# Attention plus mixer on one core: head by feature halves, feature-permuted u, keys and values of batches 4 to 7 summed over two DMAs, 8 KB rows of w_ch2, and a new order of all steps

## The chip, the core and the metric

The kernel runs on one core of a Trainium2 chip. A core has engines with a queue of their own each: TensorE (PE in the profile, its weight loads PEld), VectorE (DVE), ScalarE (ACT), GpSimd (POOL) and SyncE (SP). Matrix products land in PSUM, from where DVE or ACT move them on; DMAs move data between HBM and SBUF and are issued here from SP, ACT and POOL. Within an engine instructions run in program order; between engines they wait on semaphores. The metric is the device time of one execution in microseconds (us), lower is better.

## What is computed

```
k_p, v_p = k, v averaged over groups of 8 rows           # 576 -> 72 rows, per head
x   = softmax(q k_p^T / 8) v_p, heads side by side       # [8 batches, 576, 512]
h   = relu(x^T w_tok1) w_tok2                            # token mixing, 256 hidden
u   = x + h^T
out = u + relu(u w_ch1) w_ch2                            # channel mixing, 1536 hidden
```

q, k and v are [8, 8, 576, 64], w_tok1 [576, 256], w_tok2 [256, 576], w_ch1 [512, 1536], w_ch2 [1536, 512]; all are fp32 in HBM and bf16 in SBUF.

## The kernel before

**Units.** The program has a head and nine units. The head brings in the first data and takes batch 0 through attention and token mixing. Unit n (0 to 7) does the channel mixing of rows 0 to 511 of batch n, and unit 8 that of the last 64 rows of all batches together (`u_tails`). Each unit is a Python generator that yields after every few matmuls: a first stage of 12 tiles (`l1_tile`, L515: four matmuls 128x512 each, then a ReLU on ACT into `GT`, L519), two yields a tile, slots 0 to 23; then a second stage. In units 0 to 2 (`unit_plain`) that is 48 matmuls 128x512 (L538), with the residual added on DVE (L544). From unit 3 on (`unit_fast`) it is a product of seven block products with 84 matmuls 128x256 (L587), which needs sums of weight blocks (`weight_sum`, steps W, L558/L565) and of blocks of `GT` (`g_sums`, steps =), made on DVE, and adds with `plus` (L608).

**Order by hand.** At each yield, `unit` looks into `PLANS[n]` and issues the steps listed for that slot: steps of batch n+1 without a mark, of batch n with `<`, of batch n+2 with `>`. The text of the plan therefore is the order on all engines; the queue of each engine is in that order. `HEAD` is the same for batch 0. The steps:

- `lk lv lq` load keys, values, queries on the queue of POOL; `+k +v` issue one more accumulating DMA (`add_rows`, L140).
- `K0 K1 V0 V1` pool keys and values on POOL, `k1`, `v0`, `v1` on DVE. Batches 1 to 3 add eight rows in three operations (`pool8`, L203, L204, L207/L209). For batches 4 to 7 (`SUMMED = 4`) the rows are added by the DMAs: four DMAs a tensor, each of which brings a pair of the eight rows to fp32 sums in SBUF, and one DVE/POOL addition is left (L255). A DMA adds to what the one before it wrote, so POOL waits for each before it issues the next.
- `kpT` transposes the pooled keys on PE (L261), `Q0 Q1` transpose queries on DVE (L310), `s0` to `s3` are scores and exponentials (L321, L327), `av0` to `av4` attention times values and the division (L359, L371, L377), `at0 at1` the first token product and its ReLU (L405, L396), `u0` to `u4` the second and the sum u (L420, L421).
- u must be turned before the first stage: on PE for early batches (`t0` to `t4`, L430, L431); later through HBM: `M0 M2 M4` spill u and `M` reads it back in another order (both on SP's queue), `T0` to `T4` finish with block transposes on DVE (L453).

Batch 0 is different: keys and values are pooled on PE with the identity as weights (L270, L292), the head waits for nothing but its loads, u is turned by accumulating x and the token product transposed (`X0..3`, `A0..3`, L469, L477), and `d` steps are matmuls on a zero tile that keep PE busy (L662).

**Buffers.** PSUM pools: `ps_one` four one-bank tiles, `ps_two` two two-bank tiles. Raw keys, values, queries: two buffers each.

**u's layout.** Feature 4m+k of u stands at column 4m+k. `w_ch1` is loaded with four neighbouring rows on one partition, so the k-th quarter of the contraction is every fourth column of u.

Of the kernel before, what the change touches and what calls it, by code (L numbers as in the profile page):

```python
# [8 lines left out]
FP32 = mybir.dt.float32  # L9
# [6 lines left out]
FAST = 3  # L16
POOLE = mybir.EngineType.Pool
# [5 lines left out]
HEAD = """c0 c1 d8 q0 d1 q1 d5 kp0 kp1 kt0 d2 o0 e0 kt1 kp2 kp3 o1 e1 kt2 kt3 q2 q3 d2 o2 e2 vpool0 o3 d1 vpool1 e3 d2  # L23
          aw1 av0 av2 d2 av3 at_0 at_2 av4 at_1 at_3 d2 at_4 X0 X1 X2 A0 A1 A2 X3 A3 d3"""
PLANS = {
    0: {0: "K0", 1: "<u0", 4: "<u3", 5: "k1 Q1", 12: "V0", 15: "<u1 lv2", 18: "kpT", 19: "Q0 s2 v1",
        20: "<u2 lq3 s0", 22: "s3", 24: "s1", 25: "lv3", 26: "av1", 27: "av3 av2", 29: "lk3 av0", 30: ">K1",
        33: "av4", 34: "at1", 35: "at0", 36: "u4", 37: "u3 u2", 38: "u1", 39: ">K0 t4", 42: "t1", 43: "u0",
        44: "t2 t3", 45: "t0 >V1 >V0"},
    1: {0: "kpT", 1: "lk3", 2: "Q1", 4: "Q0", 8: "s0", 9: "lv3", 11: "s1", 14: "s2", 18: "s3", 19: ">K0", 20: "av1",  # L30
        21: "av3 >Q1", 23: "+k3a +v3a", 24: "av2", 26: "av0", 28: "av4", 29: ">K1", 30: "at1 +k3b at0",
        31: ">kpT >v0", 33: ">s2", 34: ">Q0 u0", 35: "u1", 37: "+v3b", 38: ">s3 u3", 40: "lq3 t1 t3", 41: "+k3c",
        42: ">V1 u2", 43: "lk4 +v3c", 44: ">s0 t2", 46: "t0", 47: ">s1"},
    2: {2: "av4 >K1", 3: "av3 >K0", 6: "av2 lv3", 8: "+k3a lq3", 10: "av0", 12: "av1", 13: ">Q0 >kpT", 14: "at1",
        16: "at0 >Q1", 18: "+v3a >s0", 19: "u3", 20: ">s2", 25: "u1 >V0", 26: "W00", 27: "t3 t1 >s1", 28: "W01 u0",
        29: "W02 +k3b u4", 30: "W10 u2", 32: "W03 >s3", 33: ">V1", 37: "+v3b >av0 >av2", 38: "t0", 39: "t2 >av4 W11",
        41: "W13", 43: "+k3c", 45: ">av1", 46: ">av3 t4", 47: "+v3c lv4"},
    3: {0: "lk3 >Q1", 1: ">K1 W12", 3: "at1", 5: ">K0", 9: "at0", 10: ">kpT", 11: "u3", 12: "u1 >s2", 13: "u0",
        14: "M0 >Q0", 15: "u2 M2", 16: "M +v3a lq3", 17: ">V0", 18: ">s1 =1a =2a", 22: "=3b", 23: "=1b =2b",
        25: ">s3 =4a", 27: ">V1 +v3b", 28: ">s0", 29: "+k3a", 31: "=4b", 32: "=3a >av2", 36: ">av1", 37: "+k3b",  # L40
        39: ">av0 T2", 40: "T1 T0 T3", 43: ">av4 >av3"},
    4: {1: ">Q1", 4: "+v2c at0", 5: "+k2c at1", 6: "lv3", 7: ">K0 u4 M4 >K1 lk3", 8: "u2 u3 M2 u0", 10: ">Q0",
        11: "u1", 12: ">kpT +v3a", 14: ">s2", 17: ">s1", 19: "+k3a M0", 20: "=1a =2a", 21: ">s3", 22: "=4a =3a",
        25: "=1b", 26: ">V0 M", 27: "=2b >s0", 29: "+v3b", 30: "=4b =3b", 31: ">V1", 33: ">av0", 35: "T1 lq3 >av1",
        36: ">av2 T0 T2", 37: "+k3b", 39: "T3", 43: "+k3c", 44: ">av3"},
    5: {2: "<T4 av4", 5: ">Q1 >K1", 6: "at0 at1", 8: ">K0 +v2c", 10: "u0 u1", 11: "u3", 12: ">kpT >Q0", 14: "M0",
        15: ">s2", 16: "u2 M2", 17: "=3a >s1", 18: "=1a", 19: "M =2a", 21: ">V1", 25: "=3b >s3 =1b =2b", 28: "=4a",
        29: "=4b", 31: ">s0", 33: "T2", 34: ">V0 >av0", 35: ">av1", 38: "T1", 39: ">av2 T0", 40: "T3", 41: ">av3",
        43: ">av4"},
    6: {4: "at0", 5: "at1", 6: "u4", 7: "u0 u2 u1", 8: "u3", 9: "M4", 10: "M2", 12: "M0", 14: "=3a", 16: "=3b",  # L50
        17: "M", 18: "=1a", 19: "=2a", 21: "=4a", 25: "=1b", 31: "=2b", 32: "T2 =4b", 34: "T1", 37: "T3", 39: "T0",
        44: "T4"},
    7: {7: "=3a", 16: "=3b", 19: "=1a =2a", 21: "=4a", 27: "=1b =2b", 36: "=4b"},
    8: {7: "=3a", 17: "=1a", 18: "=2a", 19: "=4a", 22: "=3b", 24: "=1b", 26: "=2b", 30: "=4b"},
# [4 lines left out]
def kernel(  # L59
# [45 lines left out]
    w_ch1 = singles.tile([P, 4, DC], BF16)  # L105
# [26 lines left out]
    def pair_sums(b, key):  # L132
        return loaded[b, key].rearrange("j h i d -> j (h i d)").bitcast(FP32)[:, 0:H * 2 * D].rearrange(
            "j (h n) -> j h n", h=H)

    def add_rows(b, key):
        i = parts_of[b, key]
        parts_of[b, key] = i + 1
        src = (k if key == "k" else v)[b].rearrange("h (j i) d -> j h (i d)", i=POOL)
        nc.gpsimd.dma_start(out=pair_sums(b, key), in_=src[:, :, 2 * i * D:2 * (i + 1) * D],  # L140
                            accum_op=ALU.add if i else ALU.bypass)
# [12 lines left out]

    def load_q(b):
        qb = loaded[b, "q"] = raw.tile([P, HP, BR * D + D], BF16, name="qb")
        if b == 0:
            nc.vector.memset(qb[:, :, BR * D:], 0.0)
            nc.gpsimd.dma_start(out=qb[:, 2:HP, 0:BR * D], in_=q_pairs(2, HP))
        else:  # L160
            nc.gpsimd.dma_start(out=quarters(qb), in_=q[b].rearrange("(g l) (j n) d -> (l j) g (n d)", l=4, n=2 * BR))
# [8 lines left out]
    def load_tok():  # L170
        nc.gpsimd.dma_start(out=f2, in_=moe_w_tok2.rearrange("(c p) n -> p c n", p=P))
        w = moe_w_tok1.rearrange("(p r) n -> p r n", r=BR)
        for half in range(2):
            rows = slice(half * BP, (half + 1) * BP)
            nc.gpsimd.dma_start(out=w_tok1[rows, 0:4, :],
                                in_=w[:, 0:8, :].rearrange("p (c u) n -> p c u n", u=2)[:, :, half])
        for half in range(2):
            rows = slice(half * BP, (half + 1) * BP)
            nc.gpsimd.dma_start(out=w_tok1[rows, 4 + half, :], in_=w[:, 8, :])

    def permute_tok2():
        src = f2.rearrange("t m (p r) -> t m r p", r=BR)
        dst = w_tok2.rearrange("t m (r p) -> t m r p", p=BP)
        for m in range(2):
            nc.gpsimd.tensor_copy(out=dst[:, m], in_=src[:, m])
# [3 lines left out]
    def load_ch1():  # L189
        for g in range(3):  # L190
            cols = slice(g * 512, (g + 1) * 512)
            nc.gpsimd.dma_start(out=w_ch1[:, :, cols], in_=moe_w_ch1[:, cols].rearrange("(p c) n -> p c n", c=4))

    def load_ch2(gs):
        for g in gs:
            nc.gpsimd.dma_start(out=w_ch2[:, 4 * g:4 * g + 4, :],
                                in_=moe_w_ch2[g * 512:(g + 1) * 512, :].rearrange("(c p) n -> p c n", p=P))
# [13 lines left out]
    tails = {}  # L211

    def batch_steps(b):
# [26 lines left out]
        def parts(src):  # L240
            return src.rearrange("p (m k) -> p k m", k=4)

        def pool(eng, t, g):
            def go():
# [5 lines left out]
                pair = pair_sums(b, t)[:, hs].rearrange("j l (i n) -> i j l n", i=2)  # L250
# [14 lines left out]
        def kp2(a):  # L265
            def go():
# [6 lines left out]
                (nc.scalar.copy if a == 1 else nc.vector.tensor_copy)(out=kpz[:, hs, 0:4:3, :], in_=view)  # L273
            return go

        def kt2(a):
            def go():
# [6 lines left out]
                nc.vector.tensor_copy(out=kT[:, :, 2 * a * SP:(2 * a + 2) * SP], in_=ps.rearrange("m o h j -> m o (h j)"))  # L284
            return go

        def ppool(g):
            def go():
                ps = ps_one.tile([P, 512], FP32, name="p1")
                hs = slice(g * HP, (g + 1) * HP)  # L290
                for i in range(POOL):
                    nc.tensor.matmul(out=ps[0:SP, 0:HP * D], lhsT=ident[0:SP, 0:SP], rhs=loaded[b, "v"][:, hs, i, :],  # L292
                                     start=(i == 0), stop=(i == POOL - 1))
                view = ps[0:SP, 0:HP * D].rearrange("j (h d) -> j h d", d=D)
                nc.vector.tensor_copy(out=st["vp"][:, hs, 0:D], in_=view)
# [50 lines left out]
        def av(c, act=False):  # L346
            def go():
# [5 lines left out]
                if first and c == 2:  # L353
                    halves = [ps_one.tile([P, 512], FP32, name="p1") for _ in range(2)]
                else:
                    ps = ps_two.tile([P, 2, 512], FP32, name="p2")
                    halves = [ps[:, 0], ps[:, 1]]
                for h in range(H):
                    nc.tensor.matmul(out=halves[h // 4][:, (h % 4) * (D + 1):(h % 4 + 1) * (D + 1)],  # L359
                                     lhsT=st["ex"][:, h * S + n0:h * S + n0 + P], rhs=st["vp"][:, h, :],  # L360
                                     start=True, stop=True)
                if first and c == 2:
                    for a in range(2):
                        view = halves[a][:, 0:4 * (D + 1)].rearrange("p (h e) -> p h e", e=D + 1)
# [388 lines left out]
```

## Time and profile before

| | before |
|---|---|
| median of 3 runs | 280.47 us (278.95 to 281.81) |
| the profiled execution | 280.81 us, of which the span in the profile is 279.0 us |
| PE, DVE, ACT, POOL busy | 264.5, 172.6, 113.4, 119.5 us |
| DMA | 37.47 MB landed, HBM read 38.21 MB |
| q0 (DMAs issued by POOL) | 32112 packets, 55.4% of 16 engines |

The span is what the profile covers; 1.8 us of the execution lie outside it. "Busy" of PE includes the latency of each matmul, so that short gaps between matmuls do not show in it. The first weight load of the first stage stands in the timeline at 24.81 us, and those of units 1 to 8 at 58.90, 90.28, 121.35, 148.26, 177.59, 208.72, 233.50 and 253.55 us; they cut the span into head and units. A line of a timeline is: start, length, engine, line and operation, out<-in, shape, count, and in brackets the idle time before it and what ended it. A line of the waits is: who waited, for whom, us in total, times, longest.

### The profile page before, as it was taken

The numbers are of one execution on the slowest core, as the hardware profiler recorded it, in microseconds if no ns is written. First come the engines' busy times: TensorE is split into PE (matmuls) and PEld (weight loads), VectorE is DVE, ScalarE is ACT, GpSimd is POOL, SyncE is SP. The second block draws the span as 40 slices with busy tenths as digits, with TensorE's granted clock in tenths as the row PEclk, the third lists the DMA queues.
The fourth block names the chain that finished last, engine by engine and source line by source line (L and its number), as shares of the span: only waits on it lengthen the run. The fifth ranks groups of instructions, "written<-read, shape, count | busy, mean of one in ns | idle before, by whom it ended". The sixth has DMA issues, their size and how long they took to land.

```text
span 279.0 us, 5000 instructions
## 1 busy us (share of the span) xinstructions
PE 264.5 (95%) x1994; PEld 150.0 (54%) x2020; DVE 172.6 (62%) x340; ACT 113.4 (41%) x200; POOL 119.5 (43%) x116
## 2 busy tenths in 40 slices
PE   8989989999999999999998999988999999999991
PEld 3755425453544544554584448632684486486581
DVE  5464986560766545783687659943895576364371
ACT  2544671129433664126711482244514422613600
POOL 8694896999959835616242446023200000000000
PEclk9999999999999999999999999997999999999999
DMA  7999999975779998989969999974406343104005
GB/s 158 194 202 207 203 202 194 214 152 119 84 86 200 173 164 100 124 175 135 166 119 144 229 167 170 164 152 59 115 0 154 109 79 85 68 0 121 31 2 150
DMA packets 49895, 37.47 MB, mean 134 GB/s; under 512 B 17424, under 2 KB 42896, under 8 KB 49872
## 3 DMA queue, kind: packets, MB, share of 16 engines
q0 software_dynamic: 32112, 22.40, 55.4%
q1 hardware_dynamic: 17440, 14.49, 20.1%
q8 instruction: 16, 0.26, 0.4%
q10 hardware_dynamic: 320, 0.26, 0.3%
q14 instruction: 7, 0.06, 0.1%
HBM read 38.21 MB, written 11.80 MB: 179 GB/s over the span
## 4 chain that ended last, share of the span: by engine, by line
PE 46%; DMA 34%; POOL 8%; issue 6%; DVE 4%; ACT 1%; POOLq 0%
DMA kr<-in_k_dram 24%; PE p L515 17%; PE p L587 13%; DMA vr<-in_v_dram 10%; PE p L538 4%; PE p L420 2%; POOL vr L140 2%; PE p L321 2%; POOL kp L255 2%; PE p L405 2%; POOL kr L140 1%; PE p L359 1%; DVE t L203 1%; POOL t L204 1%; PE p L339 1%
## 5 line engine op out<-in xcount | busy, mean ns | idle before, releaser
L519 ACT ACTIVATE GT<-p 128x512 bf16<-128x512 f32 x108 | 63.9, 597 | 97.4 <-PE p L515 81.8
L515 PE MATMUL p<-uT,w_ch 128*128 128x512 bf16 x369 | 94.2, 387 | 2.5 <-DVE uT L453 1.2
L515 PEld LDWEIGHTS <-w_ch 128*128 128x128 bf16 x432 | 39.9, 98 | 50.3 <-issue 6.6
L327 ACT ACTIVATE ex<-p 72x576 bf16<-72x576 f32 x56 | 33.2, 643 | 21.1 <-PE p L321 21.0
L538 PE MATMUL p<-w_ch,GT 128*128 128x512 bf16 x139 | 37.0, 379 | 0.4 <-issue 0.2
L140 POOL DMA_DIRECT2D kr<-in_k_dram x16 | 21.8, 1364 | 31.7 <-DMA kr<-in_k_dram 31.7
L421 DVE TENSOR_TENSOR u<-p,x 128x512 bf16<-128x512 f32 x32 | 21.3, 685 | 19.0 <-PE p L420 18.8
L140 POOL DMA_DIRECT2D vr<-in_v_dram x16 | 21.4, 1374 | 19.1 <-DMA vr<-in_v_dram 18.9
L587 PEld LDWEIGHTS <-area 128*128 128x128 bf16 x288 | 27.6, 98 | 3.3 <-issue 0.2
L587 PE MATMUL p<-area,area 128*128 128x256 bf16 x216 | 26.5, 273 | 0.0
L587 PEld LDWEIGHTS <-GT 128*128 128x128 bf16 x216 | 20.5, 98 | 4.6 <-issue 0.9
L377 DVE TENSOR_TENSOR x<-p,den 128x512 bf16<-128x512 f32 x30 | 20.7, 692 | 1.0
L538 PEld LDWEIGHTS <-GT 128*128 128x128 bf16 x144 | 12.6, 98 | 12.3 <-issue 0.9
L359 PEld LDWEIGHTS <-ex 72*128 72x128 bf16 x320 | 14.9, 98 | 6.7 <-DVE x L377 1.3
L608 DVE TENSOR_TENSOR o<-p,s 128x512 f32<-128x512 f32 (+1 forms) x24 | 15.3, 661 | 4.9 <-PE p L587 4.9
L420 PE MATMUL p<-AT,w_tok 128*128 128x512 bf16 x64 | 18.0, 379 | 0.0
L371 DVE RECIPROCAL den<-p 128x8 f32<-128x8 f32 (+1 forms) x39 | 7.8, 199 | 16.2 <-PE p L359 15.7
L396 ACT ACTIVATE AT<-p 128x512 bf16<-128x512 f32 x15 | 9.0, 597 | 21.3 <-PE p L405 18.5
L565 DVE TENSOR_TENSOR area<-GT 128x768 bf16<-128x768 bf16 x12 | 7.0, 580 | 16.9 <-ACT GT L519 16.9
L587 PE MATMUL p<-w_ch,GT 128*128 128x256 bf16 x144 | 17.4, 273 | 0.0
L359 PE MATMUL p<-vp,ex 72*128 72x65 bf16 x320 | 16.4, 194 | 0.8 <-DVE x L377 0.7
L608 DVE TENSOR_TENSOR s<-p,u 128x512 f32<-128x512 f32 x20 | 13.6, 682 | 3.6 <-PE p L587 3.6
(104 smaller groups left out, 330.9 us busy)
## 6 DMA issues: line engine op xcount, KB each, us to landing
out_dram<-o SPq DMA_DIRECT2D x34, 256.0 KB, 3.7
kr<-in_k_dram POOLq DMA_DIRECT2D x16, 288.0 KB, 6.5
vr<-in_v_dram POOLq DMA_DIRECT2D x16, 288.0 KB, 7.3
qb<-in_q_dram POOLq DMA_DIRECT2D x7, 576.0 KB, 10.3
w_ch<-in_moe_w_ch_dram POOLq DMA_DIRECT2D x6, 512.0 KB, 13.4
mem<-u SPq DMA_DIRECT2D x8, 256.0 KB, 2.4
kr<-in_k_dram POOLq DMA_DIRECT2D x3, 576.0 KB, 19.1
vr<-in_v_dram POOLq DMA_DIRECT2D x3, 576.0 KB, 14.7
```

The source lines that it names most:

```text
L140: nc.gpsimd.dma_start(out=pair_sums(b, key), in_=src[:, :, 2 * i * D:2 * (i + 1) * D], accum_op=ALU.add if i else ALU.bypass)
L327: nc.scalar.activation(out=exv[:, h:h + 2], in_=pss[a][0:SP, :, 0:SH], func=AF.Exp, scale=scale)
L359: nc.tensor.matmul(out=halves[h // 4][:, (h % 4) * (D + 1):(h % 4 + 1) * (D + 1)], lhsT=st["ex"][:, h * S + n0:h * S + n0 + P], rhs=st["vp ...
L377: nc.vector.tensor_tensor(out=dst.rearrange("p (a h d) -> p a h d", a=2, d=D), in0=view[:, :, :, 0:D], in1=den[rows, :, :, None].broadcast ...
L396: nc.scalar.activation(out=late("AT")[:, m, :], in_=ps, func=AF.Relu)
L420: nc.tensor.matmul(out=ps, lhsT=w, rhs=a, start=(i == 0), stop=(i == len(mms) - 1))
L421: nc.vector.tensor_tensor(out=dst, in0=ps, in1=x, op=ALU.add)
L515: nc.tensor.matmul(out=ps, lhsT=w_ch1[:, kk, m * P:(m + 1) * P], rhs=uT[kk], start=(kk == 0), stop=(kk == 3))
L519: nc.scalar.activation(out=GT[:, m, :], in_=ps, func=AF.Relu)
L538: nc.tensor.matmul(out=ps, lhsT=GT[:, m, c * P:(c + 1) * P], rhs=w_ch2[:, m, :], start=(m == 0), stop=(m == NM - 1))
L587: nc.tensor.matmul(out=ps[i] if split else ps[:, i], lhsT=a(m)[:, i * P:(i + 1) * P], rhs=w(m), start=start and m == 0 and (i == 0 or spli ...
L608: nc.vector.tensor_tensor(out=out[:, i], in0=ps[i] if type(ps) is list else ps[:, i], in1=other[:, i], op=ALU.add)
```

## The change

1. **Head.** Batch 0's attention times values is done by halves of the features (heads 0 to 3, then 4 to 7), two row chunks at a time, with the division on DVE or ACT; the first token product, its ReLU and the turned sum follow by halves. The filler matmuls are cut from 28 to 18. Loads are issued in another order: the 8 odd key rows before the identity is made, a part of w_tok1 before the values, batch 1's keys before w_ch1, batch 1's queries and values between the thirds of w_ch1. One half of w_tok2 is permuted on ACT. u0 of batch 0 is in the head.
2. **Keys of batch 1** are pooled on PE (`kq0 kq1`) instead of on POOL and DVE.
3. **u is stored feature-permuted**: feature 128k+m stands at column 4m+k. DVE writes u with a step of four elements (8 bytes) and reads it so in the residual additions. `w_ch1` is loaded with rows 128 apart; the k-th quarter of x and of the token product is contiguous.
4. **w_ch2 in rows of 8 KB**: each partition takes four neighbouring rows. So that the hidden units match, the weights of the first stage are read from `w_ch1` with a step of four columns.
5. **Two DMAs for batches 4 to 7**: each brings four of the eight rows (`4 * D`), the second adds to the first. Two additions are left on POOL where one was.
6. **First stage of unit 0** starts with the first halves of three tiles (`EARLY = 3`); its second stage does eight of twelve terms for two outputs before the last four.
7. **All steps in a new order** (`HEAD`, `PLANS`). Loads are issued further ahead: `+k4a` and `lk4` stand for batch n+4.

```diff
+EARLY = 3
+HEAD = """z Z Lk8 I Lk0 Lk1 Lq La R0 Lv8 Lv0 d8 Lv1 Lc d1 c0 Lf c1 Lb d2 d5 Bk1 H0 q0 d2 kP0 kp1 kt0 Bq1 o0 q1 P0
+          kt1 kp2 kp3 R1 e0 o1 kt2 kt3 q2 e1 o2 e2 q3 vp0 o3 e3 vp1 a00 a01 b10 P1 H1 Bv1 H2 a12 G0 y00 a02 y01 y02
+          y03 a11 y04 X0 y10 X1 y11 y12 y13 y14 X2 A0 A1 A2 X3 G1 Ld A3 u0"""
...
+    0: {0: "<u2", 1: "kq1 kq0", 2: "lk2 !G2 Q0", 4: "kpT", 5: "Q1 <u1 !P2", 7: "s2", 10: "V0 lq2 s0 <u3", 12: "s3",
+        13: "lv2", 15: "s1", 22: "v1 av1", 23: "av3", 24: "lk3", 25: "av2 av0", 28: "av4 lq3", 29: ">K1",
+        30: "at1 at0 >K0", 31: "u4 u3", 33: "u2", 36: "u1", 39: "lv4 >Q0 >V1 t2 >V0 lk4 t1 u0", 40: ">kpT",
+        41: "t3 >s0", 42: "t4", 45: "t0", 46: ">s1"},
...
+    4: {0: "lq3", 1: "u0 u4", 2: ">K1 >K0 M4 >kpT >Q1", 4: ">Q0", 5: "lv3 +v3a", 8: "=3a +v2a u1 u3 M0", 9: ">V0",
+        17: ">V1", 20: "=1a =2a", 23: "=4a =1b", 28: "M2 =2b =3b M", 29: ">s2", 32: "=4b T3", 33: ">s1", 34: "T2",
+        36: "+k3a >s3 T0 T1", 43: ">s0"},
+    5: {1: "av0 >K0", 2: ">Q1 av1", 4: "av2", 7: "av3", 8: "av4 >K1 >kpT >V1", 11: "at0", 12: "at1", 14: ">Q0 u1",
...
-        return loaded[b, key].rearrange("j h i d -> j (h i d)").bitcast(FP32)[:, 0:H * 2 * D].rearrange(
+        return loaded[b, key].rearrange("j h i d -> j (h i d)").bitcast(FP32)[:, 0:H * 4 * D].rearrange(
...
-        nc.gpsimd.dma_start(out=pair_sums(b, key), in_=src[:, :, 2 * i * D:2 * (i + 1) * D],
+        nc.gpsimd.dma_start(out=pair_sums(b, key), in_=src[:, :, 4 * i * D:4 * (i + 1) * D],
                             accum_op=ALU.add if i else ALU.bypass)
...
+        nc.gpsimd.dma_start(out=w_ch1[g], in_=moe_w_ch1[:, cols].rearrange("(c p) n -> p c n", p=P))
...
+                            in_=moe_w_ch2[g * 512:(g + 1) * 512, :].rearrange("(p c) n -> p c n", c=4))
...
-                pair = pair_sums(b, t)[:, hs].rearrange("j l (i n) -> i j l n", i=2)
+                four = pair_sums(b, t)[:, hs].rearrange("j l (i n) -> i j l n", i=2)
+                eng.tensor_tensor(out=four[0], in0=four[0], in1=four[1], op=ALU.add)
+                pair = four[0].rearrange("j l (i n) -> i j l n", i=2)
...
+        def at_half(g, c):
+            def go():
+                cols = slice(256 * g, 256 * (g + 1))
+                if c == 0:
+                    st["at", g] = ps_one.tile([P, 2, 256], FP32, name="p1")
+                ps = st["at", g]
                 for m in range(2):
+                    nc.tensor.matmul(out=ps[:, m], lhsT=w_tok1[:, c if c < 4 else 4 + par, m * P:(m + 1) * P],
+                                     rhs=st["x"][:, c, cols] if c < 4 else st["xt"][:, cols],
+                                     start=(c == 0 and m == 0), stop=(c == 4), skip_group_check=True)
+                if c == 4:
+                    nc.scalar.activation(out=late("AT")[:, :, cols], in_=ps, func=AF.Relu)
...
-                nc.vector.tensor_tensor(out=dst, in0=ps, in1=x, op=ALU.add)
+                nc.vector.tensor_tensor(out=parts(dst), in0=blocked(ps), in1=blocked(x), op=ALU.add)
...
+    def l1_tiles(u, ms):
+        ps = {}
+        for part in range(2):
+            for m in ms:
+                if part == 0:
+                    ps[m] = ps_one.tile([P, 512], FP32, name="p1")
+                for kk in range(2 * part, 2 * part + 2):
+                    nc.tensor.matmul(out=ps[m], lhsT=w_ch1[m // 4][:, kk, m % 4:512:4], rhs=moving(u)[kk],
+                                     start=(kk == 0), stop=(kk == 3))
+                if part:
+                    nc.scalar.activation(out=GT[:, m, :], in_=ps[m], func=AF.Relu)
                 yield
...
-            nc.vector.tensor_tensor(out=o[:, c % 2], in0=ps, in1=u["u"][:, c, :], op=ALU.add)
+            nc.vector.tensor_tensor(out=blocked(o[:, c % 2]), in0=blocked(ps), in1=parts(u["u"][:, c, :]), op=ALU.add)
...
```

The new helpers: `av_half(g, j, how)` is `av` for four heads and two row chunks (steps a, b, m); `ppool(g, "k")` pools keys on PE as it did values (`kq`); `parts` splits 512 columns into every fourth, `blocked` into four contiguous blocks.

## The prediction

> **What bounds the kernel now.** I read the page's busy rows and slices first, then the table of windows cut at the units, the waits, and the timelines of PE and POOL at the places that these name.
>
> ```profile
> PE 264.5 (95%) x1994; PEld 150.0 (54%) x2020; DVE 172.6 (62%) x340; ACT 113.4 (41%) x200; POOL 119.5 (43%) x116
> ...
> PEclk9999999999999999999999999997999999999999
> DMA  7999999975779998989969999974406343104005
> ```
>
> PE is busy in 95% of the span, so time can only come from PE: fewer matmuls, or its gaps. DMA is full in the first 55 us and again from 85 to 190 us; one slice has a granted clock of 0.7. The table of windows (one row a unit: us, then busy us of PE, PEld, DVE, ACT, POOL, clock, DMA) shows where the gaps are:
>
> ```profile
> 24.81:58.90 34.09, 32.68 (x219) 15.59 (x222) 25.07 (x37) 13.10 (x23) 27.09 (x20) 1.00 1.21 203
> ...
> 90.28:121.35 31.07, 30.69 (x252) 15.69 (x254) 19.86 (x44) 13.62 (x24) 18.05 (x18) 1.00 0.96 143
> 121.35:148.26 26.91, 26.70 (x226) 16.37 (x227) 16.47 (x35) 12.76 (x22) 9.24 (x8) 1.00 0.90 147
> 148.26:177.59 29.33, 27.99 (x223) 16.48 (x223) 22.95 (x46) 12.45 (x22) 12.57 (x12) 1.00 1.01 175
> 177.59:208.72 31.13, 28.89 (x238) 16.67 (x237) 20.70 (x41) 12.74 (x22) 6.40 (x6) 0.95 0.49 95
> ```
>
> I count each unit's matmuls in program order and give each its issue step: 216 ns for 512 columns (the chain: four of L420 in 0.86 us), 109 ns for 256 (84 of L587 in 9.17 us), 33 to 56 ns for small ones (timeline). That demand is 31.0, 29.6, 30.6, 26.6, 27.2, 26.8, 24.8, 20.0, 19.5 us for units 0 to 8, 236.1 in all, and the units take 248.9 (24.81 to PE's end at 273.7). So 12.8 us are gaps: 3.1 in unit 0, 1.8 in unit 1, 2.1 in unit 4, 4.3 in unit 5, the rest small. The waits name them:
>
> ```profile
> PE p L261 <- POOL kp L255: 2.0, 1, 2.0
> PE p L515 <- DVE uT L453: 1.2, 1, 1.2
> ```
>
> and POOL's timeline says why the pooled keys of batch 7 were late: the four DMAs that sum them go one after the other, POOL waiting each time.
>
> ```profile
> 164.51 1.42 POOL L140 DMA_DIRECT2D kr<-in_k_dram  x1 [2.85 <-DMA kr<-in_k_dram]
> 172.58 1.39 POOL L140 DMA_DIRECT2D kr<-in_k_dram  x1 [2.05 <-DMA kr<-in_k_dram]
> 181.90 1.38 POOL L140 DMA_DIRECT2D kr<-in_k_dram  x1 [7.93 <-DMA kr<-in_k_dram]
> 187.66 1.63 POOL L255 TENSOR_TENSOR kp<-kr 72x256 bf16<-72x256 f32 x2 [4.38 <-DMA kr<-in_k_dram]
> ```
>
> PE stood for 2.2 us before their transposes at 189.34, and unit 5's clock of 0.95 is another 31.1 x 0.05 = 1.6 us.
>
> **Matmul count.** 16 matmuls 128x256 are new (kq, keys of batch 1): 16 x 109 ns = +1.75 us in unit 0. The halves of the first token product cost nothing (20 x 109 ns for 10 x 216). Ten fillers fewer stand where PE waits anyway.
>
> **Weights by a step of four columns** (432 loads). Rows that read weights so already are the transposes of u (L430, 113 ns) against 98 ns contiguous; they hide under matmuls of 216 ns. Beside a moving operand that is itself read by steps (units 3 to 7, already 226 ns a matmul) no row shows it: 0 to another 10 ns x 240 = 2.4 us. I take 0, since 113 leaves 100 ns.
>
> **u by a step of 8 bytes.** 36 writes and some 40 reads on DVE. Nearest rows: L421 at 685 ns contiguous from PSUM; and on DVE
>
> ```profile
> L209 DVE TENSOR_TENSOR vp<-t 72x256 bf16<-72x256 f32 x2 | 1.3, 630 | 0.1
> ...
> L207 DVE TENSOR_TENSOR kp<-t 72x256 bf16<-72x256 f32 x1 | 0.9, 949 | 0.0
> ```
>
> the second reads by steps of 8 bytes, but beside a busy POOL. So 0 to 0.32 us each; I take 0, because at 256 elements 420 ns is what an undisturbed DVE needs (L366, 425) and both rows carry a wait. [...]
>
> **Head** (24.81 to the first L515). The keys' first DMA is issued about 1.1 us later (the small key DMA and the identity come first; 0.5 to 0.6 us each on POOL), but it then has to share the engines with less: the first L270, at 7.48, comes at 7.3 to 8.2. From there the eight exponentials (593 and 693 ns) bind, with PE in order; before the last ended at 16.58, now I get 15.8, as three PE groups stand between them instead of fillers. Then DVE: two divisions of 0.2 + 0.69, three reciprocals, two half tails of 0.6, the last half 0.89, from about 16.3 to 20.4. ACT has eight small products (1.75 together in the timeline), the permutation of w_tok2 (0.67, like L665) and the first ReLU (0.6), ending at 21.3; that is the step that sets it. Then A0, A1, A2, X3, A3 (1.95) and u0 (0.43): first L515 at 23.8, with one u done that came later. Gain 1.0 + 0.4 = **1.4 us**; bounds -0.5 and 2.5.
>
> **Weights arrive in time?** Keys of batch 1 landed at 28.8 (9.3 MB of HBM reads issued up to them), those of batch 2 at 46.1 (14.8 MB): 2 us plus bytes at 345 GB/s. In the new order that gives 22.1 us for the first third of w_ch1 (wanted 23.8), 25.6 for batch 1's queries (25.5), 28.6 and 35 for the other thirds (30.5, 36), 41 for two thirds of w_ch2 (42), 48 for the last (49). All fit, by about 1 us.
>
> **Unit 0** loses the 5.7 us on DVE of batch 1's keys:
>
> ```profile
> 28.86 3.15 DVE L203 TENSOR_TENSOR t<-kr 72x1024 f32<-72x1024 bf16 x1
> 32.04 1.64 DVE L204 TENSOR_TENSOR t<-t 72x512 f32<-72x512 f32 x1
> 33.72 0.95 DVE L207 TENSOR_TENSOR kp<-t 72x256 bf16<-72x256 f32 x1
> ```
>
> and gets two copies of 0.42. The scores no longer wait for these. Of the 3.1 us of gaps I take back 1.6 (0 to 3.1); in unit 1, 0.5 of 1.8.
>
> **Two DMAs instead of four.** 24 accumulating DMAs become 8, their packets 13,824 of 512 B become 4,608 of 1 KB. The page gives q0 32112 packets and 55.4% of 16 engines, 77 ns each. By count 9,216 go: 44 us of all engines between 60 and 190 us; by bytes nothing goes; I take half. A landing took 6.5 to 7.3 us for 288 KB; for 576 KB it lies between that and 14.6; I take 9. POOL pays one more addition of 1.27 us (L204) for each of 16 halves, 20 us, and saves 16 issues of 0.87, 14 us. Adding along POOL's new order from 77 us (keys of batch 3 pooled, as before): additions, issues and six waits of up to 9 us bring batch 7's keys to about 165 us, and PE wants them at 178. So the 2.2 us wait goes, and with it, I take, the clock drop: **-3.8 us** in unit 5. In unit 4, T0 came late because the spill's read-back landed late in a full stretch of DMAs; the new order leaves it 2.5 us more: **-1.2 us**.
>
> **New waits.** An order packed to a margin of 1 us leaves something: units 1 and 2 keep 0.5 to 1.8 now. I add 1.5 (0 to 5).
>
> **Sum** against the profiled execution: 280.8 - 1.4 + 1.75 - 1.6 - 0.5 - 3.8 - 1.2 + 1.5 = 275.5; the median of the runs shown is 0.3 lower than that execution, so **275.2 us**.
>
> **Two rules weighed.** The chip's row for the clock: a drop for one window after 2 us of idle PE in unit 5. [...]
>
> The row for POOL against DVE: DVE's L203 took 3.15 us beside POOL's L203, 1.18 at 36.76, where POOL's own L204 went from 1.27 to 2.33. [...] It speaks against the change: 16 more additions on POOL of 1.27 us can each hold up a DVE sum; up to 20 us of DVE time, of which DVE at 62% can swallow most.
>
> **Rivals.**
> - *The clock drop stays* (0.10): keys in time, but half a window at half clock somewhere, as before: 275.2 + 1.6 = 276.8.
> - *Weights come late* (0.15): at 310 GB/s instead of 345 the last parts of w_ch1 and w_ch2 are 4 to 5 us later, 1 us of it covered: +3.5, 278.7. For it: DMA share over 1 there. Against: 8 KB rows ask for fewer packets.
> - *DVE pays for steps and locks* (0.10): 76 x 0.32 = 24 us on DVE, five in a row between the ReLU and the spill of each unit; about 0.5 us a unit on the path: +3.7, 278.9. The gains of the keys would then about vanish.
> - *Slower: the doubled accumulate takes doubled time* (0.10). Place: transposes of batch 7's keys, unit 5. Six waits on POOL stand in a row before it, and the margin is 13 us; from a landing of 11 us on, each further us costs PE up to 6. At 13.5 us: 6 x 4.5 - 13 = 14 at most, of which batches 5 and 6 share slack; I take +10: 285.
> - Forecast (0.55).
>
> **Range.** The forecast's terms move it by about 3.5 to either side; the two rivals near 279 belong in: 271.7 to 280.5. About 1% (2.8 us) is what a measurement of this kernel can tell from no change. Faster: forecast, the clock case and a little of the rest, 0.70; within 1%: 0.20; slower 0.10.
>
> **What would show it.** First L515 near 23.8; kq's matmuls (16 more at the identity line); weight loads of the first stage at 113 ns and its matmuls still 216 and 226; DVE's u sums still 685; POOL's waits for keys a third as many; no wait of PE for pooled keys and clock 1.00 in unit 5; unit 0 near 34. I am wrong if unit 0 or 1 is longer than before, or the accumulating DMAs land after 11 us.

## The result, and the profile after

The changed kernel takes **293.83 us** (median of 4 runs, 292.47 to 294.86) against 280.76 us (278.95 to 281.81, 4 runs) of the kernel before on the same chip: a ratio of 1.047, 95% interval 1.0391 to 1.0548. It is slower by 13 us where 5 us less were forecast (275.2, range 271.7 to 280.5). The spans of the profiled executions are 291.1 and 279.0 us.

The page of the kernel after, busy rows and slices:

```profile
PE 268.1 (92%) x2036; PEld 158.7 (55%) x2036; DVE 189.2 (65%) x338; ACT 115.7 (40%) x202; POOL 111.3 (38%) x112
...
PEclk9999999999999999999998799999999999999999
DMA  8999999937879992799595197050235043403105
```

PE went from 95% to 92% of a longer span, and DVE has 16.6 us more to do (172.6 before), although the change takes all work on batch 1's keys from it but two copies. The table of windows, cut at the first weight load of each unit as in the prediction, for units 0, 1, 3, 4 and 5 (us, then busy us of PE, PEld, DVE, ACT, POOL, clock, DMA):

```profile
24.58:61.78 37.20, 35.11 (x258) 17.94 (x257) 24.48 (x41) 13.94 (x26) 26.27 (x24) 1.00 1.04 194
61.78:95.01 33.23, 30.59 (x231) 15.06 (x230) 22.56 (x33) 16.08 (x28) 30.77 (x26) 1.00 0.81 152
...
126.37:165.62 39.25, 31.91 (x248) 19.11 (x245) 26.26 (x48) 13.64 (x24) 14.55 (x13) 0.91 0.72 139
165.62:190.75 25.13, 24.65 (x181) 15.01 (x179) 20.83 (x31) 10.97 (x19) 9.18 (x8) 1.00 0.56 118
190.75:218.95 28.20, 27.88 (x237) 17.38 (x234) 21.89 (x42) 13.64 (x24) 0.00 (x0) 1.00 0.30 76
```

The new order also moves work between units, so a unit's length alone says little. I counted PE's demand again by the issue steps of the prediction: 33.1, 29.1, 30.1, 29.4, 23.5, 26.8, 25.8, 20.0, 19.5 us for units 0 to 8, 237.4 in all against 236.1 before. What is left of each unit is gaps:

| unit | 0 | 1 | 2 | 3 | 4 | 5 | 6 |
|---|---|---|---|---|---|---|---|
| gaps before, us | 3.1 | 1.8 | 0.5 | 0.3 | 2.1 | 4.3 | 0 |
| gaps after, us | 4.1 | 4.1 | 1.2 | 9.9 | 1.6 | 1.4 | 0.7 |

So 1.3 us are new matmuls and nearly 11 us are new gaps in units 0 to 6: 9.6 of them in unit 3, 2.3 in unit 1, 1.0 in unit 0, while unit 5 gave back 2.9. Unit 8 takes 1.1 us more as well (PE waits 0.9 us there for a sum of `GT` blocks), and what follows PE's last product 1.0 us less. Two things stand out in the profile.

**DVE's sum u takes twice as long.** The groups of the kernel after: the sums that write u by a step of 8 bytes (L446; 685 ns at L421 before), the residual additions that read u by such a step (L589; 683 ns at L544 before), and the first stage's weight loads:

```profile
L446 DVE TENSOR_TENSOR u<-p,x 128x512 bf16<-128x512 f32 x32 | 40.8, 1320 | 12.3 <-PE p L445 12.2
L589 DVE TENSOR_TENSOR o<-p,u 128x512 f32<-128x512 f32 x12 | 8.3, 692 | 5.8 <-PE p L581 5.8
L550 PEld LDWEIGHTS <-w_ch 128*128 128x128 bf16 x432 | 46.4, 114 | 42.3 <-issue 4.4
```

Writing costs 0.635 us more, times 36 sums (with the four of `u_tails`) 22.9 us of DVE. Reading costs nothing (692 against 683 ns). The weight loads are the 113 ns that were forecast.

**Unit 3 stands on the spill's read-back.** DVE's timeline there and PE's, then that of the queues of SP and POOL (start, length, issue, count; in brackets the wait before it):

```profile
151.42 0.69 DVE L660 TENSOR_TENSOR s<-p,u 128x512 f32<-128x512 f32 x1
159.80 0.45 DVE L478 STREAM_TRANSPOSE uT<-v 128x256 uint32<-128x256 uint32 x1 [7.69 <-DMA v<-mem]
160.17 0.77 DVE L603 TENSOR_TENSOR area<-GT,area 128x768 bf16<-128x768 bf16 x1
```

```profile
160.99 1.25 PE L630 MATMUL p<-w_ch,area 128*128 128x256 bf16 x5 [6.48 <-DVE area L603]
```

```profile
144.87 5.56 SPq L471 DMA_DIRECT2D v<-mem  x4
```

```profile
143.54 2.80 POOL L137 DMA_DIRECT2D vr<-in_v_dram  x2 [7.14 <-DMA vr<-in_v_dram]
159.26 1.26 POOL L258 TENSOR_TENSOR vr<-vr 72x512 f32<-72x512 f32 x1 [12.91 <-DMA vr<-in_v_dram]
```

A block transpose (T0, the first of the four, L478) waits 7.7 us on DVE for the read-back, a sum of `GT` blocks (L603) is queued behind it, and PE waits 6.5 us for that sum; then the clock is at half from 157.6 to 164.4 us. The read-back was issued from 144.87 on, just after two accumulating DMAs of values (143.54); the second of them and the last piece of the read-back land at 159.2 and 159.7. From issue to landing the last piece took 11.7 us, where the kernel before needed 4.5.

### The profile page after: what moved, and what is told of

The parts are those of the page before. It is cut to its first block, busy times and chain, and to the rows that moved or that the text cites. A ratio compares the mean times of both kernels' runs of the same rounds, so it can differ in the third digit from the quotient of the medians.

```text
span 291.1 us, 5057 instructions
## 1 busy us (share of the span) xinstructions
PE 268.1 (92%) x2036; PEld 158.7 (55%) x2036; DVE 189.2 (65%) x338; ACT 115.7 (40%) x202; POOL 111.3 (38%) x112
## 4 chain that ended last, share of the span: by engine, by line
PE 71%; DVE 15%; DMA 7%; issue 3%; ACT 1%; SPq 1%; POOL 0%; DVEq 0%; POOLq 0%
PE p L550 29%; PE p L630 17%; PE p L581 6%; DVE u L446 6%; DMA v<-mem 4%; PE p L445 4%; PE p L430 4%; PE p L334 3%; PE p L368 3%; DMA kr<-in_k_dram 2%; DVE area L603 2%; DVE u_tails L446 1%; DMA mem<-u 1%; SPq L471 1%; DVE o L589 1%
## 5 line engine op out<-in xcount | busy, mean ns | idle before, releaser
L550 PEld LDWEIGHTS <-w_ch 128*128 128x128 bf16 x432 | 46.4, 114 | 42.3 <-issue 4.4
L446 DVE TENSOR_TENSOR u<-p,x 128x512 bf16<-128x512 f32 x32 | 40.8, 1320 | 12.3 <-PE p L445 12.2
L340 ACT ACTIVATE ex<-p 72x576 bf16<-72x576 f32 x56 | 33.1, 643 | 38.3 <-PE p L334 38.1
L630 PEld LDWEIGHTS <-area 128*128 128x128 bf16 x288 | 28.6, 101 | 13.7 <-DVE area L603 8.0
L373 DVE TENSOR_TENSOR x<-p,den 128x512 bf16<-128x512 f32 x28 | 19.4, 692 | 1.0
L610 DVE TENSOR_TENSOR area<-GT 128x768 bf16<-128x768 bf16 x12 | 8.1, 678 | 15.6 <-ACT GT L553 15.6
L258 POOL TENSOR_TENSOR vr<-vr 72x512 f32<-72x512 f32 x8 | 11.7, 1468 | 12.9 <-DMA vr<-in_v_dram 12.9
L368 PEld LDWEIGHTS <-ex 72*128 72x128 bf16 x280 | 12.7, 98 | 6.7 <-DVE x L373 0.8
L137 POOL DMA_DIRECT2D kr<-in_k_dram x8 | 10.7, 1342 | 14.5 <-DMA kr<-in_k_dram 14.5
L630 PE MATMUL p<-w_ch,area 128*128 128x256 bf16 x72 | 10.1, 297 | 6.5 <-DVE area L603 6.5
L334 PE MATMUL p<-qD,kD 32*72 32x288 bf16 x224 | 12.8, 297 | 2.9 <-DVE kD L272 2.9
## 6 DMA issues: line engine op xcount, KB each, us to landing
kr<-in_k_dram POOLq DMA_DIRECT2D x11, 576.0 KB, 10.2
vr<-in_v_dram POOLq DMA_DIRECT2D x11, 576.0 KB, 11.6
```

What stands on the lines that cost most here:

```text
L258: eng.tensor_tensor(out=four[0], in0=four[0], in1=four[1], op=ALU.add)
L334: nc.tensor.matmul(out=pss[l // 2][0:SP, l % 2, 0:SH], lhsT=st["kD"][quad, g, db, :], rhs=st["qD"][quad, g, half * SH:(half + 1) * SH, db] ...
L340: nc.scalar.activation(out=exv[:, h:h + 2], in_=pss[a][0:SP, :, 0:SH], func=AF.Exp, scale=scale)
L368: nc.tensor.matmul(out=ps[:, h // 4, (h % 4) * (D + 1):(h % 4 + 1) * (D + 1)], lhsT=st["ex"][:, h * S + n0:h * S + n0 + P], rhs=st["vp"][: ...
L373: nc.vector.tensor_tensor(out=dst.rearrange("p (a h d) -> p a h d", a=2, d=D), in0=view[:, :, :, 0:D], in1=den[rows, :, :, None].broadcast ...
L446: nc.vector.tensor_tensor(out=parts(dst), in0=blocked(ps), in1=blocked(x), op=ALU.add)
```

## The experiments

Theory **W**: writing u by a step of 8 bytes is the main cause. Rival **O**: the new order and the doubled accumulating DMAs are the cause, and DVE would have room for the longer sums. Each run has the kernel before beside it on its chip; ratios are to that.

### u written in stored order, u undone, u alone, batch 4 turned on PE

Four kernels on one chip. The first keeps u's layout and lets DVE go through the columns in the order in which they are stored:

```diff
-nc.vector.tensor_tensor(out=parts(dst), in0=blocked(ps), in1=blocked(x), op=ALU.add)
+nc.vector.tensor_tensor(out=dst.rearrange("p (m k) -> p m k", k=4),
+                        in0=ps.rearrange("p (k m) -> p m k", k=4),
+                        in1=x.rearrange("p (k m) -> p m k", k=4), op=ALU.add)
```

> The changed kernel, but the sum u goes through its columns in the order in which they are stored: DVE writes contiguously and reads PSUM and x by steps of 128 elements. Layout of u and all other steps stay. Theory W (the write by a step of 8 bytes is the main cause): if reading by steps is free, the 36 sums fall from 1320 to about 690 ns, DVE loses 23 us, units 0, 1 and 3 get shorter, 283 to 286 us. Rival O (the new order and the doubled accumulates are the cause, DVE has room for the longer sums): sums at 690, but still 290 us or more. If a read by 512 bytes from PSUM costs as much as the write did, the sums stay near 1300 and the run tells nothing on W against O.

Measured: 291.62 us, ratio 1.0415 (1.0338 to 1.0492). The group of the sums:

```profile
L446 DVE TENSOR_TENSOR u<-p,x 128x512 bf16<-128x512 f32 x32 | 32.8, 1042 | 15.7 <-PE p L445 15.4
```

Reading by steps isn't free here: the sums lost 0.28 of the 0.635 us, and the time 2.2 us. That settles nothing between W and O. The second undoes part 3 (the residual additions read contiguously again as well):

```diff
-in_=moe_w_ch1[:, cols].rearrange("(c p) n -> p c n", p=P)
+in_=moe_w_ch1[:, cols].rearrange("(p c) n -> p c n", c=4)
...
-nc.vector.tensor_tensor(out=parts(dst), in0=blocked(ps), in1=blocked(x), op=ALU.add)
+nc.vector.tensor_tensor(out=dst, in0=ps, in1=x, op=ALU.add)
...
-y03 a11 y04 X0 y10 X1 y11 y12 y13 y14 X2
+y03 a11 y04 y10 y11 y12 X0 X1 y13 y14 X2
```

> The changed kernel with part 3 undone: u stored as before, w_ch1 loaded with four neighbouring rows on a partition, the first stage's turned x read by steps; in the head X0 and X1 come three products later, since they now need all features. Theory W: sums at 690 ns, 283 to 286 us. Rival O: 290 us or more. The difference to the run with u written in stored order is the cost of reading by steps, if any.

Measured: 288.32 us, ratio 1.0287 (1.0189 to 1.0385). The sums are back at 688 ns and 5.5 us are gone, 2.8 of them in unit 0 (34.4 us, and the kernel before has 34.1). But this falls short of W's 283 to 286, because unit 3 did not get shorter at all: 40.1 us. SP's queue and DVE there:

```profile
141.41 4.84 SPq L471 DMA_DIRECT2D v<-mem  x4
```

```profile
156.34 0.45 DVE L478 STREAM_TRANSPOSE uT<-v 128x256 uint32<-128x256 uint32 x1 [9.60 <-DMA v<-mem]
```

The spill goes out sooner, the read-back is issued 3.5 us sooner, and it lands no earlier after its issue: 13.3 us for its last piece. DVE and PE only wait longer for it (PE stands 8.8 us). So neither W nor O is the whole story. The third puts part 3 alone into the kernel before (same edits, and the reads by steps in the residual additions):

> The kernel before with part 3 alone (u stored feature-permuted, written by steps of 8 bytes). Theory W: sums at 1320 ns, 23 us more on DVE, five in a row on the way to each unit's first stage: 284 to 290 us, units 0 to 3 longer. Rival O: sums at 1320 ns but hidden, 280 to 282 us.

Measured: 290.57 us, ratio 1.0404 (1.0274 to 1.0534).

```profile
L424 DVE TENSOR_TENSOR u<-p,x 128x512 bf16<-128x512 f32 x32 | 39.8, 1316 | 15.2 <-PE p L423 15.2
```

**Part 3 alone makes the kernel before 10 us slower**, spread over the units: 1.3 us in unit 0, 1.5, 2.1, 0.2, 1.8, 1.1 and 1.2 in units 1 to 6. O is refuted for the order of the kernel before. The fourth takes the spill and the read-back of batch 4 out of the changed kernel:

```diff
-18: "=1a", 19: "M0", 20: "=2a", 22: "W12 lq3", 23: "=1b M2 M", ... 34: "T0 >at0 >at1 lk4 =4a", ... 40: "T3 lv3 T2", 43: "T1 >u2"
+18: "=1a", 20: "=2a", 22: "W12 lq3", 23: "=1b", ... 34: "t0 >at0 >at1 lk4 =4a", ... 40: "t3 lv3 t2", 43: "t1 >u2"
```

> The changed kernel, but batch 4's u is turned on PE (16 transposes and four DVE copies) where the spill and its read-back with four DVE block transposes stood. If the late read-back (DVE standing 7.7 us before a block transpose, PE 6.6 us behind it, then half clock) is what makes unit 3 39.2 us long, unit 3 comes to 31 to 33 us and the time to 286 to 288. If DVE's load alone makes it long, unit 3 stays above 36 and the time at 291 or more.

Measured: 287.30 us, ratio 1.0261 (1.0178 to 1.0345). Unit 3, in the table of windows:

```profile
128.04:160.60 32.56, 30.62 (x259) 19.24 (x261) 26.16 (x48) 13.61 (x24) 12.47 (x12) 1.00 0.62 116
```

39.25 us became 32.56, with the clock back at 1.00, while the sums are as long as ever. The read-back is a cause of its own, worth 6.5 us.

### Both mends, and what makes the read-back late

The fifth has u as before and batch 4 turned on PE:

> Both mends in the changed kernel: u stored as before, and batch 4 turned on PE. If the two causes add up: 293.8 - 5.5 - 6.5 = 281.8 us; if they were two sides of one wait (each hidden behind the other), 286 to 287; if taking one uncovers the other, since u plain gave nothing in unit 3 itself, 279 to 281.

Measured: **278.45 us, ratio 0.9893 (0.9841 to 0.9945)**: 15.4 us below the changed kernel, and about 1% below the kernel before. The two mends give 5.5 and 6.5 us alone and 15.4 together. In the profiled executions the excess is 4.1 us, in two places. In unit 3 it is 2.2: with the read-back left in, the shorter sums gain nothing there. In unit 1 it is 1.9: with the long sums left in, PE's gap there brought half clock when batch 4 was on PE (34.9 us), and with both mends it did not (32.1). The units in us (head: up to the first weight load of unit 0):

| | head | 0 | 1 | 2 | 3 | 4 | 5 | 6 |
|---|---|---|---|---|---|---|---|---|
| before | 24.8 | 34.1 | 31.4 | 31.1 | 26.9 | 29.3 | 31.1 | 24.8 |
| after | 24.6 | 37.2 | 33.2 | 31.4 | 39.2 | 25.1 | 28.2 | 26.5 |
| u as before | 24.6 | 34.4 | 32.4 | 30.8 | 40.1 | 24.3 | 27.7 | 26.0 |
| batch 4 on PE | 24.6 | 37.2 | 34.9 | 31.4 | 32.6 | 24.8 | 28.2 | 26.5 |
| both | 24.8 | 34.4 | 32.1 | 30.8 | 31.2 | 23.8 | 27.7 | 26.0 |

Why the read-back is late was tried by leaving out the accumulating DMAs beside it, in the kernel with u as before:

```diff
-5: "lv3 +v3a", 8: "=3a +v2a u1 u3 M0"
+5: "lv3", 8: "=3a u1 u3 M0"
```

These steps stand in the plan of unit 4, but POOL, whose queue runs ahead of PE's, issues them while PE is still in unit 3.

> The changed kernel with u stored as before, and the second DMAs of the values of batches 6 and 7 (those that run beside batch 4's read-back) left out, so four of the eight rows are missing from these values. Theory C (the doubled accumulating DMA slows the read-back down): the read-back lands in 5 us or less where it took 13.3, unit 3 falls from 40.1 to 31 to 34, the time to 280 to 283. Rival: the read-back is late by itself (its 256 B packets), it still takes over 9 us and unit 3 stays above 37.

Three of its four executions took 283.1 to 283.2 us and one 278.4; the profile is of one of the three, and its unit 1 is disturbed (a gap of 3.3 us and half clock), so only unit 3 is read from it. The window of unit 3, then what DVE waited there:

```profile
127.01:157.92 30.91, 30.00 (x244) 18.33 (x246) 24.87 (x48) 13.62 (x24) 19.15 (x18) 1.00 0.75 154
```

```profile
153.66 0.45 DVE L478 STREAM_TRANSPOSE uT<-v 128x256 uint32<-128x256 uint32 x1 [1.02 <-DMA v<-mem]
```

Unit 3 is 30.9 us instead of 40.1, DVE waits 1.0 us instead of 9.6, and the read-back's last piece takes 5.6 us instead of 13.3. It isn't quite the 5 us forecast, because POOL, now free, issues the keys' accumulating DMA at 141.6, and that one still runs beside it. The DMAs' packets show the same from the other side: in the kernel before, the 2048 packets of 256 B of this read-back ran from 143.2 to 147.8 us, most of them in a hole between accumulating DMAs; in the kernel with u as before they are interleaved with the 1,152 packets of 1 KB of the two accumulating DMAs, from 142.4 to 155.9. **The accumulating DMAs beside the read-back make it late.** What about them does it is not shown: that they accumulate, the size of their packets, their bytes, or that they are issued just ahead of the read-back. The seventh asks the same of the kernel before: part 5 alone, with the accumulating DMA where the first of three stood.

```diff
-in_=src[:, :, 2 * i * D:2 * (i + 1) * D]
+in_=src[:, :, 4 * i * D:4 * (i + 1) * D]
...
-23: "+k3a +v3a", ... 30: "at1 +k3b at0", ... 37: "+v3b", ... 41: "+k3c", ... 43: "lk4 +v3c"
+23: "+k3a +v3a", ... 30: "at1 at0", ... 43: "lk4"
```

> The kernel before with part 5 alone: two DMAs for batches 4 to 7, two additions on POOL, the accumulating DMA where the first of three stood. As predicted: the wait for batch 7's keys and the half clock behind it go, 276 to 278 us. Rival: 1 KB packets stand in the way of the read-backs and queries here too, 280 us or more.

Measured: 289.64 us, ratio 1.028 (1.0207 to 1.0353). Units 1, 4 and 5 of its table of windows, and two of its waits:

```profile
59.04:95.81 36.77, 33.05 (x240) 14.82 (x242) 20.33 (x34) 15.81 (x28) 32.15 (x27) 0.95 0.71 138
...
154.63:190.02 35.39, 29.23 (x222) 16.84 (x222) 21.22 (x46) 12.45 (x22) 7.52 (x8) 0.90 0.38 84
190.02:217.56 27.54, 27.41 (x237) 16.52 (x237) 19.62 (x41) 12.66 (x22) 0.00 (x0) 1.00 0.28 77
```

```profile
PE p L517 <- DVE uT L455: 5.9, 1, 5.9
DVE uT L455 <- DMA v<-mem: 5.3, 1, 5.3
```

The time is on the side of the rival. Unit 5 gains 3.6 us, nearly the gain that was forecast for this part. Unit 4 loses 6.0: batch 4's read-back lands late here as well, PE waits 5.9 us for its transposes and then works at half clock. Unit 1 loses 5.4: POOL waits 2.9 and 0.3 us for the first halves of batch 4 (a landing of 9.6 us is on the chain there) ahead of pooling batch 3's keys, PE stands 2.2 us for these and then works at half clock for 3.4 us. Part 5 alone is thus a loss of 8 us in the old order. The eighth is part 4 alone:

```diff
-in_=moe_w_ch2[g * 512:(g + 1) * 512, :].rearrange("(c p) n -> p c n", p=P)
+in_=moe_w_ch2[g * 512:(g + 1) * 512, :].rearrange("(p c) n -> p c n", c=4)
...
-lhsT=w_ch1[:, kk, m * P:(m + 1) * P]
+lhsT=w_ch1[:, kk, m // 4 * 512 + m % 4:m // 4 * 512 + 512:4]
```

> The kernel before with part 4 alone: w_ch2 in rows of 8 KB, first-stage weights read by a step of four columns. As predicted: weight loads 113 ns instead of 98, hidden under matmuls of 216 and 226 ns, 279 to 281.5 us. If the longer loads are not hidden beside a moving operand that is itself read by steps, units 4 to 8 get up to 0.5 us longer each: 282 to 284.

Measured: 282.33 us, ratio 1.0013 (0.9957 to 1.0069). The time itself lies where the rival was expected, but the kernel before took as long beside it. Weight loads are 113 to 114 ns, the first stage's matmuls still 216 and 227, and units 6 and 7 are as long as before (24.8 and 20.05 us), so the loads are hidden. Units 4 and 5 of its profile are 0.9 and 1.0 us longer, with more waits of PE for turned u (3.4 us where it was 1.2). The rows of 8 KB bring no faster landing either: 13.3 us in the median for the six weight DMAs, 13.4 before.

### The price of a step, by itself

Behind the last product of the version with both mends, three rounds of DVE sums 128x512 with nothing beside them:

```diff
+nc.vector.tensor_tensor(out=GT[:, 0, :], in0=ps, in1=x, op=ALU.add)
+nc.vector.tensor_tensor(out=every(GT[:, 1, :], 2), in0=blocked(ps, 2), in1=blocked(x, 2), op=ALU.add)
...
+nc.vector.tensor_tensor(out=blocked(GT[:, 5, :], 4), in0=every(ps, 4), in1=blocked(x, 4), op=ALU.add)
+nc.vector.tensor_tensor(out=blocked(GT[:, 6, :], 4), in0=blocked(ps, 4), in1=every(x, 4), op=ALU.add)
...
```

`every(t, k)` takes the columns of t by a step of k; `ps` is fp32 in PSUM, `x` bf16 in SBUF. L782 is the plain sum, L783 to L786 write by steps of 2, 4, 8 and 32 elements, L787 reads PSUM by four, L788 x by four; L789 and L790 read PSUM and x by 128, L791 and L792 have both inputs in SBUF, with the output plain and by four, and L793 and L794 are copies from PSUM on ACT, plain and by four.

> The version with both mends and, behind its last product, three rounds of DVE sums 128x512 on undisturbed engines, to price the steps by themselves (work added, so only the rows count): output bf16 contiguous, then by steps of 4, 8, 16 and 64 bytes; PSUM read by 16 bytes; x read by 8 bytes; PSUM read by 512 bytes; x read by 256 bytes; both operands bf16 in SBUF with the output contiguous and by 8 bytes; the same two outputs on ACT. Theory W: 685 ns contiguous, 1320 by 8 bytes, the stepped read of x by 8 bytes 690. If the cost is one of partly written blocks of some size, the output by 4 bytes costs less than by 8 and beyond a step it no longer grows; if it is one per non-contiguous element, all stepped outputs cost the same 1320. The read by 512 or by 256 bytes explains the 1042 ns of the sum in stored order: one of the two costs 1040, the other 690.

The groups of these lines (busy us, then mean ns of one):

```profile
L782 DVE TENSOR_TENSOR GT<-p,w_ch 128x512 bf16<-128x512 f32 x3 | 2.1, 688 | 1.0 <-ACT GT L794 1.0
L783 DVE TENSOR_TENSOR GT<-p,w_ch 128x512 bf16<-128x512 f32 x3 | 2.1, 717 | 0.0
L784 DVE TENSOR_TENSOR GT<-p,w_ch 128x512 bf16<-128x512 f32 x3 | 3.8, 1275 | 0.0
L785 DVE TENSOR_TENSOR GT<-p,w_ch 128x512 bf16<-128x512 f32 x3 | 7.4, 2453 | 0.0
L786 DVE TENSOR_TENSOR GT<-p,w_ch 128x512 bf16<-128x512 f32 x3 | 7.8, 2586 | 0.0
L787 DVE TENSOR_TENSOR GT<-p,w_ch 128x512 bf16<-128x512 f32 x3 | 2.6, 876 | 0.0
L788 DVE TENSOR_TENSOR GT<-p,w_ch 128x512 bf16<-128x512 f32 x3 | 2.0, 670 | 0.0
L789 DVE TENSOR_TENSOR GT<-p,w_ch 128x512 bf16<-128x512 f32 x3 | 2.0, 673 | 0.0
L790 DVE TENSOR_TENSOR GT<-p,w_ch 128x512 bf16<-128x512 f32 x3 | 3.0, 995 | 0.0
L791 DVE TENSOR_TENSOR GT<-w_ch 128x512 bf16<-128x512 bf16 x3 | 1.2, 416 | 0.0
L792 DVE TENSOR_TENSOR GT<-w_ch 128x512 bf16<-128x512 bf16 x3 | 3.9, 1289 | 0.0
L793 ACT CAST GT<-p 128x512 bf16<-128x512 f32 x3 | 1.8, 586 | 39.1 <-DVE GT L790 39.1
L794 ACT CAST GT<-p 128x512 bf16<-128x512 f32 x3 | 3.9, 1291 | 0.1
```

A bf16 output by a step of 4, 8, 16 and 64 bytes costs 717, 1275, 2453 and 2586 ns against 688 contiguous (L782 to L786): almost free, 1.9 times, 3.6 times, and little more beyond. That fits the expectation's cost of partly written blocks, whose size no run shows, and not one for each non-contiguous element, by which all stepped outputs would cost the same. Reading x by 8 bytes costs nothing (L788), nor PSUM by 512 bytes (L789); PSUM by 16 bytes costs 876 (L787); and x by 256 bytes 995 (L790), which explains the 1042 ns of the sum in stored order. It isn't PSUM's doing, since with both inputs in SBUF the step makes 1289 out of 416 (L792, L791), and ACT pays as well: 1291 for 586 (L794, L793).

### Two more orders

In unit 1 of every kernel with the new order PE stands 1.9 to 3.5 us for the copy of batch 3's turned keys, behind `v0` on DVE. In the version with both mends I moved the transposes ahead of it:

```diff
-22: "W10", 23: "lk4", 26: "at0 >v0", 28: "at1", 30: ">kpT"
+22: "W10", 23: "lk4", 24: ">kpT", 26: "at0 >v0", 28: "at1"
```

> The version with both mends, and in unit 1 the transposes of batch 3's pooled keys are moved from slot 30 to slot 24, so that their copy on DVE stands before the three additions of v0 (1.2, 3.5 and 1.4 us there) and not behind them. PE waits 1.9 us for that copy. If this wait is the only thing late there: 276.5 us. Rival: the next thing behind v0 (the residual of unit 1 that frees a bank, or u0) takes its place: 278.0 to 278.5, no gain. If the keys are not pooled by slot 24, PE waits earlier: up to 279.

Measured: 276.76 us (12 runs), ratio 0.9888 (0.9847 to 0.9928), not to be told from the version without it (0.9893): the median is near the 276.5 without a rival, but the kernel before was a little faster beside it, too. The profile is of the slowest of the twelve. In it the gap of 1.9 us before the scores is gone (0.2 left), PE then waits 1.0 us for the residual behind `v0`, and unit 1 is 31.9 us instead of 32.1: the rival, as far as this one profile shows.

The last puts the four block transposes of batch 4 behind all sums of unit 3, in the kernel with u as before:

```diff
-34: "T0 >at0 >at1 lk4 =4a", 35: "W02", 40: "T3 lv3 T2", 43: "T1 >u2"
+34: ">at0 >at1 lk4 =4a", 35: "W02", 40: "lv3", 43: ">u2", 44: "T0 T3 T2 T1"
```

> The changed kernel with u stored as before, and the four block transposes of batch 4 moved behind all sums of unit 3 (slot 44). The read-back lands at 156 us as before. If it is the place on DVE that costs (sums waiting behind a transpose that waits for a DMA): PE works on until unit 3's end and then waits for the transposes only, unit 4 begins near 158.5 instead of 162.4, no half clock: 284 to 285 us. If the landing itself is all that counts, unit 4 begins at 161 or later: 287 to 288.

Measured: 286.50 us, ratio 1.0209 (1.0117 to 1.0301). Unit 4 begins 35.0 us after unit 3 instead of 40.1, but PE still stands 5.3 us, now for the transposes themselves, and unit 4 runs partly at half clock (0.90) and takes 26.8 us instead of 24.3. (Unit 1 lost 1.8 us to half clock in this execution, which the kernel that it is compared with did not.) Of the 9.2 us that the read-back costs in unit 3 (40.1 against 30.9 without the DMAs beside it) the place on DVE is the smaller part; the landing is what counts.

## Why the prediction was wrong, point by point

- **u by a step of 8 bytes: wrong, and the largest single error.** "I take 0", with bounds of 0 and 0.32 us each. Of the two rows that the bounds came from, one reads by steps; no DVE sum of before writes single elements by a step, and I let a reading stand for a writing. Measured: 0.635 us for each of the 36 writes, 0 for the 40 reads. At 8 bytes the output decides: written so, the sum takes 1275 ns instead of 688; with x read so, 670. The rival "DVE pays for steps and locks" had nearly the right sum of DVE time (24 us; 22.9 measured), by luck: 76 x 0.32, where it is 36 x 0.635 and nothing for the reads. It turned that into 0.5 us a unit on the path. In the kernel before it is 0.2 to 2.1 us a unit, 10 in all. Of the four steps of the output only the one of 4 bytes is almost free (717 ns).
- **Unit 4's T0, "the new order leaves it 2.5 us more", -1.2 us: wrong in sign.** The late read-back became 9.9 us of gaps in unit 3, 6.6 of them one stand and some 1.7 the half clock behind it (3.5 us of work between 160.9 and 164.4). I counted what is issued before the read-back, not what runs beside it.
- **Slower, "the doubled accumulate takes doubled time": the right resource at the wrong place.** A landing of 576 KB takes 10.2 us (keys) and 11.6 (values) in the median of all loads of that size; I took 9. But batch 7's keys had slack enough: unit 5 shows no wait of PE for pooled keys and a clock of 1.00. The price came due at batch 4's read-back, and in the old order also at POOL's wait ahead of batch 3's keys.
- **Unit 5, -3.8 us: nearly right.** Its gaps went from 4.3 to 1.4 us in the changed kernel, and part 5 alone in the old order takes 3.6 us from unit 5. The half clock went with the wait: unit 5's clock is 1.00 where it was 0.95 behind 1.96 us of idle PE, as the trace's row had it.
- **Unit 0, -1.6 us: right, but covered.** With u as before its gaps are 1.3 us where they were 3.1; the longer sums took it back and more. The 16 matmuls of kq are there. **Unit 1, -0.5: wrong**, 4.1 us of gaps, and still 3.0 with both mends; the wait for the turned keys behind `v0` is new.
- **Head, -1.4 us: half right.** The first weight load comes at 24.58, not 23.8. That includes u0 (0.43 by the old sums), so the gain is about 0.7.
- **Weights by a step of four columns, 0: right** (114 ns, part 4 alone changes nothing). The slower matmuls beside which no row showed it are those of units 4 to 7 (227 ns); unit 3 takes 216. **Weights in time: right**; PE's waits show none for w_ch1 or w_ch2. What rows of 8 KB should bring did not show.
- **New waits, 1.5 (0 to 5): too small.** An order packed by hand leaves more than slack when two of the durations under it are wrong. Of the signs of being wrong, the longer units 0 and 1 came (37.2 and 33.2 us), and so did landings after 11 us.
- **A reading.** PE's last product of the kernel before ends at 273.4 us, not 273.7, so its gaps are 12.5 us, not 12.8; no term of the sum rests on it.

Summed: what was forecast for the keys, unit 0 and unit 5 is in the version with both mends, which comes to 278.45, 3.2 us above the forecast. What part 5 or the order would each be worth there was not taken apart.

## What to carry to other kernels

Price a strided operand by a row that strides the same operand: an output by 8 bytes doubled a sum (1320 ns for 685) whose bf16 input could be read by 8 bytes for nothing, so at such a step it is the permutation's reader, not its writer, that should step. Where the transfer that the next stage needs is issued beside a bulk of larger packets, look at what is on the engines at its hour: here, beside two accumulating DMAs, the last piece of a read-back took 11.7 to 13.3 us instead of 4.5. And a plan with waits in program order has several bottlenecks in one place: two mends of 5.5 and 6.5 us gave 15.4 together, so test them together before calling either small.

## What the runs showed of the hardware that was not expected

- **A gap of PE of about 2 us can bring half clock, and need not.** By the profile's waits (0.1 to 0.2 us less than most of the stands above), 1.96 us in unit 5 of the kernel before were followed by 3.41 us at half clock (189.54 to 192.95), and 2.1 us in unit 1 by 3.4 us in two runs (part 5 alone, where the unit's clock is 0.95, and the late transposes, where 1.8 us were lost to it); 1.7 us (both mends), 2.0 (u as before) and 2.4 (the changed kernel) in unit 1 were followed by none. Gaps of 5.1 to 8.6 us brought 6.8 us each: the changed kernel, u as before and the late transposes at batch 4's read-back, and unit 4 with part 5 alone. So length alone does not tell. In the traces of the kernels before and after, the stretches at full and at half clock, up to a drop in the last us of the span, are whole multiples of 3.41 us: 54, 1 and 25 of them before, 45, 2 and 37 after. With each trace cut into pieces of 3.41 us from its drop, the 1.96 us lie whole in the piece that ends where the drop begins (186.13 to 189.54), and the 2.4 us in unit 1 of the changed kernel are split over two pieces, 0.65 and 1.72 us. That a gap's place decides would fit both; no run moved a gap to test it. A gap of 2 us thus cost 1.7 us more (half of 3.4) or nothing more.
- **ACT pays for a stepped bf16 output as DVE does**: by 8 bytes 1291 ns for 586, where DVE has 1275 for 688.
- **Single additions on DVE took several times as long.** In the run with the keys' transposes moved, a weight sum on DVE took 3.54 us, where the same sum took 0.54 in the version with both mends (both operands in SBUF). In that version it was the next but one, an addition of `v0` (75.23 to 78.76 us), that took 3.53 us on DVE (1.10 in the run with the transposes moved), beside one of POOL (74.91 to 78.19) that took 3.28 where its like took 2.13. Whether the one held up the other was not shown; no run took POOL's addition away.
